# First-half memory values as 32-column strips on block-diagonal probabilities, in a 64-segment recurrent attention kernel

## The chip, the core and the metric

The kernel runs on one core of a Trainium2 chip. The metric is the device time of one execution in microseconds; the engines are named as in the profile: PE is TensorE (PEld its weight loads), DVE is VectorE, ACT is ScalarE, POOL is GpSimd, SP is SyncE.

## The reference

The input x has 2048 rows of 640. It is normalized, cut into 64 segments of 32 rows, and the segments are processed one after the other. Eight memory rows stand before the 32 rows of a segment, and the eight output rows of the memory become the memory of the next segment:

```python
for s in range(n_seg):
    h = concatenate([mem, xs])                  # 8 + 32 rows of 640
    q, k, v = h @ Wq, h @ Wk, h @ Wv            # 32 heads of 128
    scores = where(mask, q @ k.T * scale, -1e9) # memory rows see all 40, tokens are causal
    o = softmax(scores) @ v @ Wo
    mem = o[:, :8]; outs.append(o[:, 8:])
```

Behind it come a residual, a second layer norm, and a feed-forward part (640 to 1728 to 640) with a squared ReLU. All tensors are bf16.

## The kernel before

All weights lie in SBUF. The order of instructions is written out by hand, and each engine works through its own queue in that order. `step(b, sp)` is one segment s = 4b + sp, with four segments to a block of 128 rows. The last eight rows of each segment (the "tails") do not feed the recurrence through the projections of the segment's main part: their q, k and v are projected for four segments together as fill work, which stands in the list `fill` and is run in places where PE would wait. Other postponed work stands in the lists `late`, `mid` and `owed`; `run(list, n)` issues from them.

One step goes as follows on PE. The rows that matter (8 memory rows and 24 tokens, `hT4`) are projected with 32-column weight loads, four of them side by side in the array's columns (k = 0 to 3 on output partitions 32k): q and k of heads' half 0 and 1 (`project`), then v in two halves (`ps0`, `ps1`, from five 128-row pieces c = 0 to 4 each). ACT brings the results out of PSUM as rows (q, k) or into `v`; DVE turns the rows (`flip`) into `qT` and `kT`. `v` has partitions (g, key), with g one of four head groups, and columns (i, e), where i is one of eight heads of a group and e the head's 128 columns.

Attention is split. The memory's eight queries are on the recurrence: `scores(n)`, for half n (four of the eight i), lets all heads share one 128x40 score tile `sm` (partitions g, j, query; `spread` puts the queries into `qz` by POOL). `soft1(n)` takes the maximum on DVE and the exponential `em` with its sum `zm` on ACT. `soft2(n)` makes the probabilities on DVE: reciprocal `rm`, `pmem` = em times rm in two instructions (the 32 main keys, and the eight tail keys spread over four j by the mask `same`), and a 32x32-block transposition to `pTm`. `values(n)` multiplies: 16 matmuls with a 32-row weight load (one g's keys of one head, 128 columns) and eight moving columns, and four for the tails (`vt4`), into the PSUM tile `po`; `values_out(n)` copies the memory part into `oT` (DVE for half 0, ACT for half 1).

The tokens' attention is one segment late: `token_scores` puts 128x320 scores into a bank `sk`; DVE and ACT make the softmax during the second part of the step (`tk`, `ek`, `zk`); POOL scales it (`pkt`, `pk`); DVE turns it in the next step (`pTt`, `pTk`, from `owed[0]` and `owed[1]`); `token_values` of segment s-1 multiplies it in the same `po` tile, and ACT copies it out in the step after (`token_out`). `tokens_kept`, on POOL, puts the tails' part aside (`owed[2]`).

Then `wo_rounds` multiplies `oT` by Wo into `pw`, in 16 rounds of four matmuls; its first six rounds need the half 0 that `values_out(0)` wrote, and the rounds enclose `token_values` and `values(1)`. `mem_to_hT` turns the memory rows of `pw` into the next segment's `hT4`.

The order around the change, on PE: `scores(0)`; v half 0, c = 0, 1; `token_scores(0)`; v half 0, c = 2 to 4; v half 1, c = 0, 1; `scores(1)`; `token_scores(1)`; v half 1, c = 2; `values(0)`; v half 1, c = 3, 4; one fill unit; `wo_rounds` 0 to 6. On DVE: `mx` of half 0, two kT flips, `soft2(0)`, `mx` of half 1, the eviction of half 0, `soft2(1)`, then the tokens' softmax.

`matmul` (L116 in the profile, for every matrix product) counts PE's instructions in `issued`, and `align` splits some projections' matmuls in two, so that the count at a given place of a step is the same modulo 256.

Of the kernel before, what the change touches and what calls it, by code (L numbers as in the profile page):

```python
# [9 lines left out]
ALU = mybir.AluOpType  # L10
AX = mybir.AxisListType
F32 = mybir.dt.float32
BF16 = mybir.dt.bfloat16
# [3 lines left out]
def kernel(  # L17
# [28 lines left out]
    NS = S // SEG  # L46
    HD = 24
    TL = SEG - HD
    NK = SEG + M
# [11 lines left out]
    const = ctx.enter_context(tc.tile_pool(name="const", bufs=1))  # L61
# [13 lines left out]
    wv = wts.tile([128, DC * HE], BF16)  # L75
    wo = wts.tile([128, H, D], BF16)

    ident = const.tile([128, 128], BF16)
    o_ring = [const.tile([64, DH], BF16, name="o%d" % k) for k in range(5)]
    o0 = const.tile([128, DC, 32], BF16, name="om")  # L80
    nc.vector.memset(o0[:], 0.0)
    make_identity(nc, ident[:])
    mhalf = const.tile([128, 1], F32)
    nc.vector.memset(mhalf[:], -0.5)
# [13 lines left out]
        nc.vector.tensor_copy(out=same[r], in_=ident[r, r].rearrange("p (j k) -> p j k", k=TL))  # L98
    nc.vector.tensor_reduce(out=diag[:], in_=same[:], op=ALU.add, axis=AX.X)
    nc.vector.tensor_copy(out=same[:], in_=diag[:].unsqueeze(2).to_broadcast([128, 4, TL]))  # L100
    qT = const.tile([128, H, NK], BF16)
    kT = const.tile([128, H, NK], BF16)
    oT = const.tile([128, H, NK], BF16)
    nc.vector.memset(oT[:], 0.0)
# [9 lines left out]
    def matmul(*a, **k):  # L114
        issued[0] += 2
        nc.tensor.matmul(*a, **k)  # L116
# [136 lines left out]
    def evac(dve, out_, in_):  # L253
        if dve:
            nc.vector.tensor_copy(out=out_, in_=in_)
        else:
            nc.scalar.copy(out=out_, in_=in_)  # L257
# [15 lines left out]
    def wo_rounds(lhs, pw, h0, h1):  # L273

        for h in range(h0, h1):
            for kh in range(2):
                for ch in range(2):
                    j = kh * 2 + ch
                    p = h // 8 * 16 + kh * 8 + h % 8
                    matmul(pw[32 * j:32 * j + 32, 0:DH], lhsT=lhs(p), rhs=wov2[:, head(p), ch],  # L280
                                     start=(h == 0), stop=(h == 15))
# [17 lines left out]
        for a in range(2):  # L299
            nc.vector.tensor_tensor(out=hT4[64 * a:64 * a + 64, :, sp, 0:M], in0=tr[0:64, a, :, 0:M], in1=tc_[:, a], op=ALU.add)  # L300

    fill, late, mid, owed = [], [], [], [[], [], []]

    def run(q, n):
        while n > 0 and q:
            q.pop(0)()
            n -= 1
# [85 lines left out]

    def mem0_to_hT(hT4):
        mt = s1.tile([128, DC, 32], BF16, tag="pk", name="mt")
        nc.vector.transpose(out=mt[:], in_=o0[:])
        nc.vector.tensor_copy(out=hT4[:, :, 0, 0:M], in_=mt[:, :, 0:M])

    def tails_in(b, sp, which="qk", h0=0, h1=H):
# [23 lines left out]
    oTg = oT[:].rearrange("p (n g j) q -> p n g j q", n=2, g=G)  # L423
    back = []

    def token_values(s, v, vt4, po, opens):

        sp = s % 4
        pTk, pTx = back.pop()
        for i in range(HG):  # L430
            for g in range(G):
                r = slice(32 * g, 32 * g + 32)
                matmul(po[:, g, i * 32:(i + 1) * 32], lhsT=v[r, i * E:(i + 1) * E], rhs=pTk[r, i, :],
                                 start=(opens and i == 0), stop=False, skip_group_check=True)
        for u in range(2):
            for g in range(G):
                r = slice(32 * g, 32 * g + 32)
                matmul(po[:, g, u * 128:(u + 1) * 128].rearrange("p (j q) -> p j q", q=32)[:, :, HD:32],
                                 lhsT=vt4[r, sp, u, :], rhs=pTx[r, u], start=False, stop=True, skip_group_check=True)
# [17 lines left out]
    prev = {}  # L457

    def step(b, sp, v=None):
# [41 lines left out]
        def soft1(n):  # L501
            mx = s2.tile([128, 1], F32, tag="mx", name="mx")
            nc.vector.tensor_reduce(out=mx[:], in_=sms[n][:, 0:NK], op=ALU.max, axis=AX.X, negate=True)  # L503
            em = s2.tile([128, NK], BF16, tag="em", name="em")
            zm = s2.tile([128, 1], F32, tag="zm", name="zm")
            nc.scalar.activation(out=em[:], in_=sms[n][:, 0:NK], func=ACT.Exp, bias=mx[:, 0:1], scale=1.0,  # L506
                                 accum_out=zm[:])
            ems[n], zms[n] = em, zm

        def soft2(n):  # L510
            rm = s2.tile([128, 1], F32, tag="rm", name="rm")
            nc.vector.reciprocal(out=rm[:], in_=zms[n][:])
# [6 lines left out]
            nc.vector.transpose(out=pT[:], in_=pm[:])  # L519
            return pT  # L520

        def values(n, pT, po):
            c0 = 256 + n * 4 * M
            for j in range(4):
                i = n * 4 + j
                for g in range(G):
                    r = slice(32 * g, 32 * g + 32)
                    matmul(po[:, g, c0 + j * M:c0 + (j + 1) * M], lhsT=v[r, i * E:(i + 1) * E],
                                     rhs=pT[r, j * M:(j + 1) * M], start=(i == 0), stop=False,
                                     skip_group_check=True)  # L530
            for g in range(G):
                r = slice(32 * g, 32 * g + 32)
                matmul(po[:, g, c0:c0 + 4 * M], lhsT=vt4[r, sp, n, :], rhs=pT[r, 32:64],
                                 start=False, stop=True, skip_group_check=True)

        def values_out(n, po):
            c0 = 256 + n * 4 * M
            evac(n == 0, oTg[:, n, :, :, 0:M], po[:, :, c0:c0 + 4 * M].rearrange("p g (j m) -> p g j m", m=M))

        if not ready and not last:  # L540
            align(s + b, 4 * 8 * DC + 32 + 1 + 16)
# [12 lines left out]
        elif not ready:  # L554
            spread(1)
        run(late, 10)
        run(owed[2], 1)

        def first_half():
            if not last:  # L560
# [23 lines left out]
            proj(wv, "half", lhs, 0, ps0, 2, DC)  # L584
            nc.scalar.copy(out=v[:, 0:512], in_=ps0[:])
        if not last:
            pT0 = soft2(0)
        if not ready:
            ps1 = mmtile()
            proj(wv, "half", lhs, 1, ps1, 0, 2)  # L590
# [2 lines left out]
        token_scores(1)  # L593
        if not last:
            soft1(1)
        if ready:
            run(fill, DC)
        po = pop.tile([128, G, 512], F32, tag="po", name="po")
        if not ready:
            proj(wv, "half", lhs, 1, ps1, 2, 3)  # L600
        if not last:
            values(0, pT0, po)
            values_out(0, po)
        if not ready:
            proj(wv, "half", lhs, 1, ps1, 3, DC)
            nc.scalar.copy(out=v[:, 512:1024], in_=ps1[:])  # L606
        if not last and len(fill) > 7:
            run(fill, 1)
# [8 lines left out]
        pw = chn.tile([128, 512], F32, tag="ch", name="pw")  # L617
        main = lambda p: oT[:, p, 0:32]
        wo_rounds(main, pw, 0, 6)
        if s:  # L620
            token_values(s - 1, prev["v"], prev["vt4"], po, last)
        if not last:
            values(1, pT1, po)
            values_out(1, po)
        wo_rounds(main, pw, 6, 8)
        run(fill, DC if ready else 1)
        wo_rounds(main, pw, 8, 12)
# [32 lines left out]
        owed[1].append(lambda: nc.vector.transpose(out=pTk[:], in_=pk[:]))  # L660
        back.append((pTk, pTx))
        if not last:
            tails_in((s + 1) // 4, (s + 1) % 4)
# [242 lines left out]
    end_output(NS - 2)  # L906
    run(late, 100)
    po = pop.tile([128, G, 512], F32, tag="po", name="po")
    token_values(NS - 1, prev["v"], prev["vt4"], po, True)
    for n in range(2):  # L910
        token_out(n, po)
    tokens_kept(NS - 1)
# [102 lines left out]
```

## Time and profile before

| what | value |
|---|---|
| median of three runs | 959.4 us (959.19 to 960.17) |
| profiled execution | 958.06 us |
| its span, first to last instruction | 956.3 us |
| granted PE clock | 1.000 |
| PE busy | 929.1 us, 97% |
| DVE busy | 699.7 us, 73% |
| ACT busy | 548.4 us, 57% |
| POOL busy | 258.2 us, 27% |

A row of the groups gives line, engine, operation, tiles (out<-in), shape and count, then busy us, mean ns of one, and idle time just before. A row of the timeline gives start and duration in us, then the same names, the count of merged instructions, and in brackets an idle time of that engine and what ended it. A shape such as 128\*32 on PE is rows by columns of the loaded weights.

### The profile page before, as it was taken

Reading aid. Unit: us, or ns where it says so; the run is one execution under the profiler, and the core shown is the slowest. Engines: PE = TensorE matmul, PEld = TensorE weight load, DVE = VectorE, ACT = ScalarE, POOL = GpSimd, SP = SyncE. Lnnn points to the kernel's source line nnn. Section 1 sums busy time; section 2 is a strip of 40 time slices with the busy share of each in tenths; the row PEclk is TensorE's granted clock in tenths of the full one; section 3 lists DMA queues with packets and bytes.
Section 4 is the critical chain, followed back from the end, with each engine's and each line's share of the span. In section 5 each row is a group of like instructions: output and inputs, shape, how many; then the busy total and the mean of one; then the engine's idle time right before and its main releaser. Section 6 shows DMA issues by size and latency. Waiting matters only on the chain.

```text
span 956.3 us, 57547 instructions
## 1 busy us (share of the span) xinstructions
PE 929.1 (97%) x25874; PEld 570.3 (60%) x25883; DVE 699.7 (73%) x2136; ACT 548.4 (57%) x1343; POOL 258.2 (27%) x798
## 2 busy tenths in 40 slices
PE   4989999999999999999999999999999998999998
PEld 2545666666666666666666666656666665555555
DVE  3167778888888888888887787878787888566532
ACT  2556666666666666666666666656666665523321
POOL 1013222222222222222222222222222233263300
PEclk9999999999999999999999999999999999999999
DMA  9973210101010101010101010101010111643320
GB/s 360 396 235 90 45 29 13 29 13 30 10 33 9 34 10 34 9 34 9 33 10 34 9 32 11 32 11 32 11 32 11 53 43 21 199 113 86 94 56 28
DMA packets 60838, 56.74 MB, mean 59 GB/s; under 512 B 27696, under 2 KB 56752, under 8 KB 58672
## 3 DMA queue, kind: packets, MB, share of 16 engines
q1 hardware_dynamic: 59712, 52.73, 18.3%
q8 instruction: 202, 3.31, 1.5%
q10 hardware_dynamic: 880, 0.34, 0.1%
q14 instruction: 44, 0.36, 0.1%
HBM read 38.37 MB, written 9.44 MB: 50 GB/s over the span
## 4 chain that ended last, share of the span: by engine, by line
PE 93%; DMA 3%; DVE 2%; ACT 1%; issue 1%; ACTq 0%; DVEq 0%
PE ps L116 63%; PE pw L116 16%; PE y L116 6%; PE po L116 5%; DMA vt_d<-row 2%; PE sm L116 1%; PE pa L116 1%; DMA om<-in_A_mem_dram 1%; ACT otc L298 0%; ACTq L157 0%; ACT row L266 0%; DVE otr L297 0%; DVE kTt L269 0%; DVE qT L269 0%; DVE kT L269 0%
## 5 line engine op out<-in xcount | busy, mean ns | idle before, releaser
L116 PEld LDWEIGHTS <-hT 128*32 128x32 bf16 x8383 | 216.9, 96 | 146.2 <-DVE hT L300 20.7
L116 PE MATMUL pw<-wo,oT 128*32 128x320 bf16 x4224 | 178.4, 300 | 0.2
L116 PE MATMUL ps<-wv,hT 128*32 128x512 bf16 x2520 | 177.5, 380 | 0.0
L116 PE MATMUL ps<-wq,hT 128*32 128x512 bf16 (+1 forms) x3168 | 160.6, 336 | 4.8 <-DVE hT L300 4.8
L116 PE MATMUL ps<-wk,hT 128*32 128x512 bf16 (+1 forms) x2575 | 159.7, 375 | 0.0
L641 POOL TENSOR_TENSOR pkt<-ek,rk 128x64 bf16<-128x64 bf16 x64 | 19.3, 301 | 421.7 <-DVE rk L639 408.4
L116 PEld LDWEIGHTS <-oT 128*32 128x32 bf16 x4224 | 100.9, 96 | 44.8 <-ACT oT L257 9.1
L269 DVE STREAM_TRANSPOSE qT<-row 128x512 bf16<-128x512 bf16 x128 | 89.5, 699 | 24.4 <-ACT row L264 20.5
L264 ACT ACTIVATE row<-ps 128x512 bf16<-128x512 f32 (+1 forms) x170 | 93.7, 562 | 13.7 <-PE ps L116 11.7
L937 ACT ACTIVATE wv<-ps,b1f 128x512 bf16<-128x512 f32 (+1 forms) x56 | 37.6, 673 | 66.5 <-PE ps L116 66.0
L442 ACT CAST oT<-po 128x512 bf16<-128x512 f32 x128 | 74.7, 586 | 0.0
L298 ACT COPY otc<-otr 64x40 f32<-64x40 f32 x126 | 28.2, 224 | 71.5 <-DVE otr L297 71.1
L453 POOL COPY qz<-qT 128x96 bf16<-128x96 bf16 x126 | 33.5, 266 | 112.5 <-DVE mx L503 58.2
L116 PEld LDWEIGHTS <-hTt 128*32 128x32 bf16 x1640 | 45.1, 97 | 31.4 <-issue 2.0
L266 ACT CAST row<-ps 128x512 bf16<-128x512 f32 (+1 forms) x113 | 61.6, 560 | 1.9 <-PE ps L116 0.5
L635 DVE TENSOR_REDUCE zk<-ek 128x8 f32<-128x320 bf16 x64 | 31.1, 486 | 42.9 <-ACT ek L633 42.9
L116 PEld LDWEIGHTS <-v 32*128 32x128 bf16 x4064 | 42.1, 91 | 32.8 <-issue 18.4
L116 PE MATMUL y<-wq,wk 128*128 128x320 bf16 x448 | 61.2, 299 | 0.2 <-DVE wk L938 0.2
L484 ACT CAST row<-ps 128x256 bf16<-128x256 f32 x126 | 40.8, 376 | 30.3 <-PE ps L116 30.2
L257 ACT CAST oT<-po 128x128 bf16<-128x128 f32 x63 | 16.8, 267 | 65.3 <-PE po L116 65.3
L606 ACT CAST v<-ps 128x512 bf16<-128x512 f32 x63 | 37.0, 587 | 29.7 <-PE ps L116 29.7
L116 PEld LDWEIGHTS <-qz 128*32 128x32 bf16 x2016 | 36.0, 95 | 28.1 <-ACT em L506 1.9
(109 smaller groups left out, 1659.9 us busy)
## 6 DMA issues: line engine op xcount, KB each, us to landing
wv<-in_A_Wv_dram SPq DMA_DIRECT2D x5, 1024.0 KB
wq<-in_A_Wq_dram SPq DMA_DIRECT2D x5, 1024.0 KB
wk<-in_A_Wk_dram SPq DMA_DIRECT2D x5, 1024.0 KB
vt<-vt_d SPq DMA_DIRECT2D x60, 64.0 KB
xt<-in_A_x_dram SPq DMA_DIRECT2D x18, 160.0 KB
wo<-in_A_Wo_dram SPq DMA_DIRECT2D x2, 1280.0 KB
wo<-in_A_Wo_dram SPq DMA_DIRECT2D x4, 640.0 KB
wq<-in_B_w_dram SPq DMA_DIRECT2D x1, 2080.0 KB
```

Source lines behind the costliest of these rows:

```text
L116: nc.tensor.matmul(*a, **k)
L264: nc.scalar.mul(out=row, in_=ps, mul=scale)
L266: nc.scalar.copy(out=row, in_=ps)
L269: nc.vector.transpose(out=dst[:, n * 16:(n + 1) * 16, 0:32], in_=row.rearrange("p (h e) -> p h e", e=32))
L298: nc.scalar.copy(out=tc_[:, a], in_=tr[64:128, a, :, 0:M])
L442: nc.scalar.copy(out=oTg[:, n, :, :, M:NK], in_=po[:, :, n * 128:(n + 1) * 128].rearrange("p g (j q) -> p g j q", q=32))
L453: nc.gpsimd.tensor_copy(out=d.rearrange("p a (j f) -> p a j f", j=3)[:, :, :, 0:M], in_=src[:, :, 0:3, :])
L484: nc.scalar.copy(out=row[:, u * 256:(u + 1) * 256], in_=ps[:, u * 256:(u + 1) * 256])
L606: nc.scalar.copy(out=v[:, 512:1024], in_=ps1[:])
L635: nc.vector.tensor_reduce(out=zk[:], in_=ek[:], op=ALU.add, axis=AX.X)
L641: nc.gpsimd.tensor_tensor(out=pkt[:], in0=ek[:, :, SEG:NK], in1=rk[:].unsqueeze(2).to_broadcast([128, HG, TL]), op=ALU.mult)
L937: nc.scalar.activation(out=r[:, 0:w], in_=ps[:, 0:w], func=ACT.Relu, bias=b1f[:, fc:fc + 1], scale=1.0)
```

## The change

Half 0 of the memory values is computed the other way round. The probabilities are laid out block-diagonally over the four head groups: `soft2_wide` multiplies them by `gmask` and `gsame`, masks that keep column group g only on the partitions of group g, into `pwide` (128 x 2 x 4 x 32: main keys and tail keys). The main part is one DVE instruction; the tail part is two POOL instructions, the second of which scales by `rm`. One DVE transposition of 256 columns gives `pTwide`. `values_wide` then loads `v` with all 128 key partitions and 32 of a head's columns at a time, and multiplies 32 moving columns: 16 matmuls, and four for the tails with 128 moving columns. They write strips of 32 partitions into columns 320 to 447 of the bank `sk`, which holds the token scores in columns 0 to 319. Its eviction to `oT` stays on DVE.

Half 1 stays as it was and loses its argument n; `po` is taken later, ahead of `token_values`. In PE's order the values now come after c = 2 and 3 of v's half 1 instead of after c = 2. The turning of `pTk` moves from `owed[1]` to a new `owed[3]`, run behind `soft1(1)`; `tokens_kept` is run behind `soft2_wide`. The first memory rows are loaded into a part of `qT` instead of a tile of their own, one output buffer is dropped, and `issued` is corrected by two in some steps.

```diff
-    o_ring = [const.tile([64, DH], BF16, name="o%d" % k) for k in range(5)]
+    o_ring = [const.tile([64, DH], BF16, name="o%d" % k) for k in range(4)]
...
+    gmask = const.tile([128, 4], BF16)
+    nc.vector.tensor_reduce(out=diag[:], in_=ident[:].rearrange("p (g k) -> p g k", k=32), op=ALU.add, axis=AX.X)
+    nc.vector.tensor_copy(out=gmask[:], in_=diag[:])
+    gsame = const.tile([128, 4, 4 * TL], BF16)
+    nc.vector.tensor_tensor(out=gsame[:], in0=same[:].rearrange("p j k -> p (j k)").unsqueeze(1).to_broadcast([128, 4, 4 * TL]),
+                            in1=gmask[:].unsqueeze(2).to_broadcast([128, 4, 4 * TL]), op=ALU.mult)
...
+        def soft2_wide(n):
+            rm = s2.tile([128, 1], F32, tag="rm", name="rm")
+            nc.vector.reciprocal(out=rm[:], in_=zms[n][:])
+            pm = s1.tile([128, 2, 4, SEG], BF16, tag="pwide", name="pwide")
+            tails_ = pm[:, 1].rearrange("p g (j k) -> p (g j) k", k=TL)
+            nc.gpsimd.tensor_tensor(out=tails_, in0=ems[n][:, SEG:NK].unsqueeze(1).to_broadcast([128, 16, TL]),
+                                    in1=gsame[:].rearrange("p g (j k) -> p (g j) k", k=TL), op=ALU.mult)
+            nc.gpsimd.tensor_tensor(out=tails_, in0=tails_, in1=rm[:].unsqueeze(2).to_broadcast([128, 16, TL]), op=ALU.mult)
+            nc.vector.scalar_tensor_tensor(out=pm[:, 0], in0=ems[n][:, 0:SEG].unsqueeze(1).to_broadcast([128, 4, SEG]),
+                                           scalar=rm[:, 0:1], in1=gmask[:].unsqueeze(2).to_broadcast([128, 4, SEG]),
+                                           op0=ALU.mult, op1=ALU.mult)
+            pT = s1.tile([128, 2, 4, SEG], BF16, tag="pTwide", name="pTwide")
+            nc.vector.transpose(out=pT[:].rearrange("p t g k -> p (t g k)"), in_=pm[:].rearrange("p t g k -> p (t g k)"))
+            return pT
+
+        def values_wide(pT, sk):
+            c0 = HG * NK
+            split = lambda x: x.rearrange("p (g j m) -> p g j m", g=G, m=M)
+            main, kept = (pT[:, t].rearrange("p g k -> p (g k)") for t in range(2))
             for j in range(4):
-                i = n * 4 + j
+                for q in range(4):
+                    r = slice(32 * q, 32 * q + 32)
+                    matmul(split(sk[r, c0:c0 + 128])[:, :, j], lhsT=v[:, j * E + 32 * q:j * E + 32 * q + 32],
+                           rhs=split(main)[:, :, j], start=False, stop=False, skip_group_check=True)
+            for q in range(4):
+                r = slice(32 * q, 32 * q + 32)
+                matmul(sk[r, c0:c0 + 128], lhsT=vt4[:, sp, 0, 32 * q:32 * q + 32], rhs=kept,
+                       start=False, stop=True, skip_group_check=True)
+            evac(True, oTg[:, 0, :, :, 0:M], split(sk[:, c0:c0 + 128]))
...
-        run(owed[2], 1)
...
-            pT0 = soft2(0)
+            pT0 = soft2_wide(0)
+        run(owed[2], 1)
...
             soft1(1)
+        run(owed[3], 1)
...
-        po = pop.tile([128, G, 512], F32, tag="po", name="po")
         if not ready:
-            proj(wv, "half", lhs, 1, ps1, 2, 3)
+            proj(wv, "half", lhs, 1, ps1, 2, 4)
         if not last:
-            values(0, pT0, po)
-            values_out(0, po)
+            values_wide(pT0, sk)
+            issued[0] += 0 if sp else 2
         if not ready:
-            proj(wv, "half", lhs, 1, ps1, 3, DC)
+            proj(wv, "half", lhs, 1, ps1, 4, DC)
...
-        owed[1].append(lambda: nc.vector.transpose(out=pTk[:], in_=pk[:]))
+        owed[3].append(lambda: nc.vector.transpose(out=pTk[:], in_=pk[:]))
```

More of the change, by code (lines that the diff above doesn't have):

```diff
@@ L78 @@
     ident = const.tile([128, 128], BF16)
-    o_ring = [const.tile([64, DH], BF16, name="o%d" % k) for k in range(5)]
-    o0 = const.tile([128, DC, 32], BF16, name="om")
-    nc.vector.memset(o0[:], 0.0)
+    o_ring = [const.tile([64, DH], BF16, name="o%d" % k) for k in range(4)]
     make_identity(nc, ident[:])
@@ L100 @@
     nc.vector.tensor_copy(out=same[:], in_=diag[:].unsqueeze(2).to_broadcast([128, 4, TL]))
+    gmask = const.tile([128, 4], BF16)
[4 more added lines that the diff above has]
+                            in1=gmask[:].unsqueeze(2).to_broadcast([128, 4, 4 * TL]), op=ALU.mult)
     qT = const.tile([128, H, NK], BF16)
+    o0 = qT[:].rearrange("p h k -> p (h k)")[:, 0:DC * 32].rearrange("p (c f) -> p c f", f=32)
+    nc.vector.memset(o0, 0.0)
     kT = const.tile([128, H, NK], BF16)
@@ L300, in mem_to_hT @@
             nc.vector.tensor_tensor(out=hT4[64 * a:64 * a + 64, :, sp, 0:M], in0=tr[0:64, a, :, 0:M], in1=tc_[:, a], op=ALU.add)
-    fill, late, mid, owed = [], [], [], [[], [], []]
+    fill, late, mid, owed = [], [], [], [[], [], [], []]
     def run(q, n):
@@ L395, in mem0_to_hT @@
         mt = s1.tile([128, DC, 32], BF16, tag="pk", name="mt")
-        nc.vector.transpose(out=mt[:], in_=o0[:])
+        nc.vector.transpose(out=mt[:], in_=o0)
         nc.vector.tensor_copy(out=hT4[:, :, 0, 0:M], in_=mt[:, :, 0:M])
@@ L424, with token_values @@
     back = []
-    def token_values(s, v, vt4, po, opens):
+    def token_values(s, v, vt4, po):
         sp = s % 4
@@ L433, in token_values @@
                 matmul(po[:, g, i * 32:(i + 1) * 32], lhsT=v[r, i * E:(i + 1) * E], rhs=pTk[r, i, :],
-                                 start=(opens and i == 0), stop=False, skip_group_check=True)
+                                 start=(i == 0), stop=False, skip_group_check=True)
         for u in range(2):
@@ L520, in soft2, with values @@
             return pT
-        def values(n, pT, po):
-            c0 = 256 + n * 4 * M
-            for j in range(4):
-                i = n * 4 + j
+        def soft2_wide(n):
[16 more added lines that the diff above has]
+            main, kept = (pT[:, t].rearrange("p g k -> p (g k)") for t in range(2))
+            for j in range(4):
+                for q in range(4):
[7 more added lines that the diff above has]
+            evac(True, oTg[:, 0, :, :, 0:M], split(sk[:, c0:c0 + 128]))
+        def values(pT, po, opens):
+            c0 = 256 + 4 * M
+            for j in range(4):
+                i = 4 + j
                 for g in range(G):
@@ L528, in values @@
                     matmul(po[:, g, c0 + j * M:c0 + (j + 1) * M], lhsT=v[r, i * E:(i + 1) * E],
-                                     rhs=pT[r, j * M:(j + 1) * M], start=(i == 0), stop=False,
+                                     rhs=pT[r, j * M:(j + 1) * M], start=(opens and j == 0), stop=False,
                                      skip_group_check=True)
@@ L532, in values @@
                 r = slice(32 * g, 32 * g + 32)
-                matmul(po[:, g, c0:c0 + 4 * M], lhsT=vt4[r, sp, n, :], rhs=pT[r, 32:64],
+                matmul(po[:, g, c0:c0 + 4 * M], lhsT=vt4[r, sp, 1, :], rhs=pT[r, 32:64],
                                  start=False, stop=True, skip_group_check=True)
-        def values_out(n, po):
-            c0 = 256 + n * 4 * M
-            evac(n == 0, oTg[:, n, :, :, 0:M], po[:, :, c0:c0 + 4 * M].rearrange("p g (j m) -> p g j m", m=M))
+            evac(False, oTg[:, 1, :, :, 0:M], po[:, :, c0:c0 + 4 * M].rearrange("p g (j m) -> p g j m", m=M))
         if not ready and not last:
@@ L619, in step @@
         wo_rounds(main, pw, 0, 6)
+        po = pop.tile([128, G, 512], F32, tag="po", name="po")
         if s:
-            token_values(s - 1, prev["v"], prev["vt4"], po, last)
+            token_values(s - 1, prev["v"], prev["vt4"], po)
         if not last:
-            values(1, pT1, po)
-            values_out(1, po)
+            values(pT1, po, s == 0)
         wo_rounds(main, pw, 6, 8)
@@ L908 @@
     po = pop.tile([128, G, 512], F32, tag="po", name="po")
-    token_values(NS - 1, prev["v"], prev["vt4"], po, True)
+    token_values(NS - 1, prev["v"], prev["vt4"], po)
     for n in range(2):
```

## The prediction

> **What bounds the kernel now.** I read the page first, then the timeline of one segment around the changed step, then the groups by form for prices.
>
> The page's busy line and its chain:
>
> ```profile
> PE 929.1 (97%) x25874; PEld 570.3 (60%) x25883; DVE 699.7 (73%) x2136; ACT 548.4 (57%) x1343; POOL 258.2 (27%) x798
> ...
> PE 93%; DMA 3%; DVE 2%; ACT 1%; issue 1%; ACTq 0%; DVEq 0%
> ```
>
> TensorE carries the chain and works through its queue in order. Whatever holds its next instruction moves the end, once in each of 62 like segments of about 12 us (of 64; the first has no value projection, the last no memory).
>
> The timeline of one segment, from the first half's exponential to the first output matmuls (weight loads show when TensorE reaches each step):
>
> ```profile
> 516.66 0.29 ACT L506 ACTIVATE em<-sm,mx 128x40 bf16<-128x40 f32 x1
> ...
> 516.86 0.19 ACT L506 ACTIVATION_READ_ACCUMULATOR em<-sm,mx 128x1 f32 x1
> 517.09 0.15 DVE L512 RECIPROCAL rm<-zm 128x1 f32<-128x1 f32 x1
> ...
> 517.69 0.12 PEld L116 LDWEIGHTS <-hT 128*32 128x32 bf16 x4
> ...
> 517.70 0.24 DVE L519 STREAM_TRANSPOSE pTm<-pmem 128x64 bf16<-128x64 bf16 x1
> 517.87 0.16 DVE L503 TENSOR_REDUCE mx<-sm 128x1 f32<-128x40 f32 x1
> 518.04 0.17 PEld L116 LDWEIGHTS <-v 32*128 32x128 bf16 x16 [0.23 <-ACT v L585]
> ...
> 518.27 0.12 PEld L116 LDWEIGHTS <-hT 128*32 128x32 bf16 x8
> ...
> 518.41 0.29 DVE L255 CAST oT<-po 128x128 bf16<-128x128 f32 x1 [0.38 <-PE po L116]
> ...
> 518.76 0.54 PEld L116 LDWEIGHTS <-oT 128*32 128x32 bf16 x13 [0.15 <-DVE oT L255]
> ```
>
> To see: em ends at 517.05; probabilities, values, eviction and first oT load follow at 518.76, 1.71 later. pTm is ready (517.94) about when TensorE wants it (518.04), and TensorE already waits 0.15 for the eviction. So this chain of small steps is as tight as TensorE's own work; nothing spare lies in it. In three other timelines em's end to oT is 1.78, 1.67 and 1.72: mean 1.72.
>
> Prices of the new operations:
>
> ```profile
> L644 POOL TENSOR_TENSOR pk<-ek,rk 128x256 bf16<-128x256 bf16 x64 | 39.8, 622 | 0.0
> ...
> L660 DVE STREAM_TRANSPOSE pTk<-pk 128x256 bf16<-128x256 bf16 x64 | 25.8, 403 | 0.0
> ...
> L641 POOL TENSOR_TENSOR pkt<-ek,rk 128x64 bf16<-128x64 bf16 x64 | 19.3, 301 | 421.7 <-DVE rk L639 408.4 <-DVE hn L744 6.7 <-ACT otmp L287 6.6
> ```
>
> To see: one POOL product costs 301 ns at 64 columns and 622 at 256, so 408 by the straight line at 128; a 256-column transposition costs 403. The hand-overs are in the opening timeline:
>
> ```profile
> 3.95 0.21 DVE L175 BATCH_NORM_AGGREGATE lnmv<-lnst 128x2 f32<-128x12 f32 x1
> ...
> 4.25 0.22 POOL L177 TENSOR_SCALAR lnrs<-lnmv 128x1 f32<-128x1 f32 x1 [2.80 <-DVE lnmv L175]
> ...
> 4.56 0.60 POOL L178 TENSOR_TENSOR lnrs<-lnrs,mhalf 128x1 f32<-128x1 f32 x1
> ...
> 5.30 0.45 DVE L191 TENSOR_SCALAR xn<-xt,lnmv,lnrs 128x640 bf16<-128x640 bf16 x1
> ```
>
> To see: into POOL 0.09 (4.16 to 4.25), POOL to a dependent POOL instruction 0.09 (4.47 to 4.56), POOL to DVE 0.14 (5.16 to 5.30).
>
> **What TensorE saves.** Both forms of the first half's memory values are 20 weight loads and 20 matmuls. Now they cost more than their issue, because the 32-row tiles follow and precede 32-column tiles: from the c=2 group (517.69) to the c=3 group (518.27) is 0.58, where like groups of four stand 0.216 apart (twenty start at 500.59, the next at 501.67). So they cost 0.36. The new strips stay in the column form; sixteen qT loads of that form take 0.14 (517.55 to 517.69), and the four tail strips, which move 128 columns, a quarter of 0.216, so 0.19 in all. Saving 0.17 a segment, 10.5 us over 62, if TensorE had nothing to wait for. The Trainium skill (TensorEngine Tiling (Array Packing), Key Properties) says that changing the tiling mode drains the engine; these gaps agree, and by that rule alone the sum would be this 10.5 us gain.
>
> **What it waits for instead.** In the new order TensorE reaches the values after c=2 and c=3: 517.69 + 2 x 0.216 = 518.12. The probabilities must now go through POOL: masked tails (needs em only), tails times 1/sum (needs the first and rm), and DVE's 256-column transposition, which waits for POOL. From em's end 517.05: 0.09 into POOL, 0.41 first product, 0.09, 0.41 second, 0.14 to DVE, 0.40 transposition, 0.05 to TensorE (hT's end 511.37 to its load 511.42) = 1.59, so 518.64. TensorE stands 0.52. DVE's own masked main part (128 columns; the 32-column form costs 246) ends before POOL does and is off this path.
>
> Then values to eviction start 0.37 as now (518.04 to 518.41; twenty pairs both times) plus 0.04 for the wider tail strips, eviction 0.29, to the oT load 0.06: 519.40. From em's end 2.35, against 1.72 on average: **0.63 later** a segment. What TensorE saved and the work that it still has (c=4 and some fill, 0.43) lies inside this, before the eviction lands. Afterwards the order is as before and nothing gives time back: the recurrence (pw, otr, hT) starts from the later output matmuls.
>
> **Behind DVE's wait** are queued the second half's maximum (0.16), the moved pTk transposition (0.40) and the eviction. Laid end to end after 518.59 they let the eviction start at 519.15 instead of 519.05; neighbours on DVE overlap by some 0.08 each (518.62 starts before 518.70), so 0 to 0.10. I take 0 and keep 0.10 (6.2 us) for the range. The second half's probabilities end 1.06 after the eviction starts (543.28 to 544.34): 520.11, while TensorE wants them at 520.20 + 0.63. The token scores' softmax shifts with the eviction, as TensorE does; its sum ended 0.25 before otr started (510.06, 510.31), and still does.
>
> **Edits at nothing.** pTk's old place (515.08 in this segment) was covered: the qT flip behind it waits for its row from ACT (514.91 plus 0.60, flip at 515.54). Only where a layer-norm step follows pTk, in one segment of four, does the flip start some 0.2 earlier, and there em still waits for ACT's two kT rows. tokens_kept (0.40 on POOL) moves behind both products; POOL is then idle for over 6 us, and the next token eviction on ACT that waits for it comes 4 us later. The strips share the token scores' bank, which is released by DVE at the same instruction as before. The po tile is taken later and its old evictions are long done. No DMA is issued or moved; 34 more waits stand in TensorE's queue for landed vt4 tiles, each a few ns. The opening adds a 128x128 product on DVE ahead of xn at 12.53, which TensorE's transpositions await: 0.3, with the mask copy 0.4 once.
>
> **Sum.** 958.06 (the profiled execution; span 956.3) + 62 x 0.63 + 0.4 = 997.5. The median 959.4 is 1.3 above the profiled one: **999 us**.
>
> **Bounds.** POOL's spans may mislead: by starts, pkt to pk is 0.25 and pk to the next 0.56, so 0.36 at 128. With that for both and hand-overs 0.1 shorter in all the delay is 0.43: 986. At POOL's shortest span (0.22) for both products it is 0.25: 975. With 0.62 for both, 1.05: 1025. I take 0.41, between its two nearest forms.
>
> **Rivals.**
> Shared port, more delay: in the feed-forward part a DVE product of two SBUF tensors takes 0.42 alone and 1.63 when POOL's product began 0.05 earlier:
>
> ```profile
> 869.16 0.42 DVE L938 TENSOR_TENSOR wk<-wv 128x512 bf16<-128x512 bf16 x1
> ...
> 869.97 1.39 POOL L749 TENSOR_TENSOR wv<-wk,wq 128x640 f32<-128x640 bf16 x1
> ...
> 870.02 1.63 DVE L938 TENSOR_TENSOR wk<-wv 128x512 bf16<-128x512 bf16 x1
> ```
>
> It ended 0.29 after POOL. Here DVE's masked main part (em and the mask, both in SBUF) would meet POOL's first product, end 0.29 after it at 517.84, and hold off the second (due 517.64) by 0.20: delay 0.83, **1011**. Against: the blocked one may give way before its end. The Trainium skill (SBUF — State Buffer, Who interferes with whom) has this as an exclusive lock held for the whole instruction; the two rows agree. Chance, with the DVE queue's 0.10 (1005): 0.22.
>
> POOL cheaper than its spans: 975 to 986, chance 0.2. POOL dearer (0.62 each): 1025, chance 0.05.
>
> Faster: TensorE's 0.17 counts because the probabilities come in time: 958.06 - 10.5 + 0.4 + 1.3 = **949**. It decides at 518.12: the transposition must reach TensorE 1.07 after em's end, where my sum has 1.59 and the floor of two shortest POOL products 1.21. Even then eviction and oT would come at 518.88, 0.12 after now (967), unless they shorten too. For it: the 0.36 is real. Chance 0.04.
>
> The change does nothing: the built order on each engine shows all of it, so only cancelling would give 959; chance 0.01.
>
> **Numbers.** 999 has 0.48 (988 to 1005). With the shared port and the dear end of the cheap case the range is 975 to 1015, leaving out the rest. A difference under 0.2% (1.9 us) can't be told here. Faster 0.04, same 0.02, slower 0.94.
>
> **What would show it.** Right: pTwide's transposition starting about 1.1 after em's end; TensorE idle about 0.5 ahead of its first strip; the eviction about 0.6 later than now; a group pwide<-em on POOL near 0.41; segments of 12.6. Wrong: strips starting at 517.69 + 0.43 on that scale without idle time, POOL products near 0.2, or the oT load less than 1.9 after em's end.

## The result and the profile after

The changed kernel takes 986.86 us (median of four runs, 986.29 to 987.22) against 959.3 us for the kernel before (four runs, 957.73 to 960.17): a ratio of 1.0289, with a 95% interval of 1.0271 to 1.0306. It is slower by 27.6 us. The profiled execution took 987.11 us with a span of 985.3 us, 29.0 more than the span before, at a granted clock of 1.000.

The busy line and the chain of the page after:

```profile
PE 939.2 (95%) x25858; PEld 564.3 (57%) x25867; DVE 720.3 (73%) x2076; ACT 546.5 (55%) x1343; POOL 307.1 (31%) x924
...
PE 76%; ACT 8%; DVE 5%; POOL 5%; DMA 2%; issue 2%; ACTq 0%; POOLq 0%; DVEq 0%
```

TensorE fell from 93% to 76% of the chain. POOL, which was not in it at all, now holds 5%, and ACT (ahead of POOL, with two kT rows and `em`) and DVE (behind it, with `pTwide`) grew. In the segment shown below the chain leaves TensorE once and goes through the softmax of half 0.

The timeline of one segment after, of the same kind as the one shown of before, from the end of the exponential to the first output matmuls:

```profile
534.81 0.19 ACT L512 ACTIVATION_READ_ACCUMULATOR em<-sm,mx 128x1 f32 x1
...
535.14 0.40 POOL L533 TENSOR_TENSOR pwide<-em,gsame 128x128 bf16<-128x128 bf16 x1 [0.46 <-ACT em L512]
...
535.23 0.46 DVE L536 SCALAR_TENSOR_TENSOR pwide<-em,rm,gmask 128x128 bf16<-128x128 bf16 x1
...
535.62 0.40 POOL L535 TENSOR_TENSOR pwide<-pwide,rm 128x128 bf16<-128x128 bf16 x1
535.65 0.15 PEld L122 LDWEIGHTS <-hT 128*32 128x32 bf16 x8
...
536.05 0.45 DVE L540 STREAM_TRANSPOSE pTwide<-pwide 128x256 bf16<-128x256 bf16 x1 [0.37 <-POOL pwide L535]
...
536.55 0.28 PE L122 MATMUL ps<-pTwide,v 128*32 128x32 bf16 x16 [0.27 <-DVE pTwide L540]
536.55 0.17 PEld L122 LDWEIGHTS <-v 128*32 128x32 bf16 x15 [0.58 <-issue]
...
536.94 0.29 DVE L261 CAST oT<-ps 128x128 bf16<-128x128 f32 x1
...
537.28 0.67 PEld L122 LDWEIGHTS <-oT 128*32 128x32 bf16 x24 [0.46 <-DVE oT L261]
537.29 1.00 PE L122 MATMUL pw<-wo,oT 128*32 128x320 bf16 x24
```

`em` ends at 535.00. The two POOL products follow each other (535.14 to 535.54, 535.62 to 536.02), the transposition starts 0.03 behind the second and ends at 536.50, and the strips start at 536.55. TensorE took up c = 2 and 3 at 535.65; at 0.216 a group it was through with them at 536.08, and the strips came 0.47 later. (The matmul records, whose ends are modelled, leave 0.27 of idle time; the weight side shows 0.58, since the first strip's weights had been loaded ahead.) The first oT load comes 2.28 after `em`'s end, where it was 1.71.

The same two last steps in the kernel before, from its timeline of that segment (`em` ended at 517.05), with the matmuls, which the prediction did not look at:

```profile
518.76 0.82 PEld L116 LDWEIGHTS <-oT 128*32 128x32 bf16 x24 [0.15 <-DVE oT L255]
...
518.92 0.99 PE L116 MATMUL pw<-wo,oT 128*32 128x320 bf16 x24
```

Before, the load ran 0.16 ahead of its matmul, because the array still had the fill unit's four matmuls to do, which started at 518.71; after, load and matmul come together (537.28, 537.29), because those four had started at 536.93. Measured to the first output matmul, the change costs 2.29 - 1.87 = 0.42 in this segment, while the loads say 0.57. Over all segments the medians of this stretch are, by place in a block of four, 1.88, 1.88, 1.88 and 1.76 before and 2.41, 2.29, 2.29 and 2.29 after: 0.41 more in the second and third place, 0.53 in the first and fourth, 0.48 on average.

The groups by form after, for the new operations:

```profile
L540 DVE STREAM_TRANSPOSE pTwide<-pwide 128x256 bf16<-128x256 bf16 x63 | 28.1, 445 | 23.7 <-POOL pwide L535 23.7
L536 DVE SCALAR_TENSOR_TENSOR pwide<-em,rm,gmask 128x128 bf16<-128x128 bf16 x63 | 27.5, 437 | 2.2
L535 POOL TENSOR_TENSOR pwide<-pwide,rm 128x128 bf16<-128x128 bf16 x63 | 25.2, 400 | 5.2 <-DVE pwide L536 0.4
L533 POOL TENSOR_TENSOR pwide<-em,gsame 128x128 bf16<-128x128 bf16 x63 | 25.2, 400 | 30.1 <-ACT em L512 29.3 <-DVE rm L530 0.8
```

The POOL products cost 400 ns each, as estimated (408). DVE waits 23.7 us in all for the second of them, 0.38 on average in 63 segments.

Where the 29.0 us of the profiled spans lie: 27.3 between the first and the last hand-over of the memory (62 segments, 0.44 each), 1.4 before the first hand-over, 0.3 behind the last. The median length of a segment, by its place in a block of four (from the end of one hand-over to the next, from segment 16 on), shows the loss in every place:

| kernel | first | second | third | fourth |
|---|---|---|---|---|
| before | 12.44 | 11.96 | 11.92 | 11.91 |
| e3, the moves only | 12.32 | 11.96 | 11.92 | 11.90 |
| after | 12.86 | 12.37 | 12.34 | 12.44 |
| e1, tails on DVE | 12.76 | 12.20 | 12.16 | 12.26 |
| e2, no tails | 12.49 | 11.93 | 11.90 | 12.00 |
| e7, transposition split | 12.49 | 12.14 | 12.11 | 12.21 |
| e5, row form on a constant | 12.32 | 11.96 | 11.92 | 11.90 |
| e6, strips on a constant | 12.45 | 11.77 | 11.73 | 11.73 |
| e9, the same with the count mended | 12.40 | 11.77 | 11.73 | 11.72 |

The first place needs care. In the profiled execution of the kernel before, its segments scatter from 12.32 to 12.80; in e3, whose time equals that of the kernel before, their median is 12.32. Against e3 the change loses 0.54, 0.41, 0.42 and 0.54, which is the 0.53, 0.41, 0.41 and 0.53 of the stretch from `em` to the first output matmul, and 0.48 on average. The 0.44 above is smaller mainly because that one execution of the kernel before had longer first segments.

### The profile page after: what moved, and what is told of

It reads as the page before. It is cut to its first block, busy times and chain, and to the rows that moved or that the text cites. A ratio compares the mean times of both kernels' runs of the same rounds, so it can differ in the third digit from the quotient of the medians.

```text
span 985.3 us, 57590 instructions
## 1 busy us (share of the span) xinstructions
PE 939.2 (95%) x25858; PEld 564.3 (57%) x25867; DVE 720.3 (73%) x2076; ACT 546.5 (55%) x1343; POOL 307.1 (31%) x924
## 4 chain that ended last, share of the span: by engine, by line
PE 76%; ACT 8%; DVE 5%; POOL 5%; DMA 2%; issue 2%; ACTq 0%; POOLq 0%; DVEq 0%
PE ps L122 49%; PE pw L122 16%; PE y L122 6%; ACT row L490 4%; PE po L122 4%; DVE pTwide L540 3%; POOL pwide L535 3%; POOL pwide L533 2%; ACT em L512 2%; DMA vt_d<-row 1%; PE pa L122 1%; DMA qT<-in_A_mem_dram 1%; DVE wk L971 0%; ACT row L272 0%; ACT otc L304 0%
## 5 line engine op out<-in xcount | busy, mean ns | idle before, releaser
L122 PEld LDWEIGHTS <-oT 128*32 128x32 bf16 x4224 | 95.9, 96 | 60.0 <-DVE oT L261 25.7
L122 PEld LDWEIGHTS <-v 32*128 32x128 bf16 (+1 forms) x4064 | 47.5, 92 | 58.7 <-issue 53.6
L970 ACT ACTIVATE wv<-ps,b1f 128x512 bf16<-128x512 f32 (+1 forms) x56 | 37.5, 672 | 66.9 <-PE ps L122 65.6
L512 ACT ACTIVATE em<-sm,mx 128x40 bf16<-128x40 f32 x126 | 37.0, 293 | 55.3 <-DVE mx L509 53.7
L275 DVE STREAM_TRANSPOSE kT<-row 128x512 bf16<-128x512 bf16 x65 | 45.5, 700 | 11.1 <-ACT row L272 11.0
```

The costliest lines, as they stand in the source:

```text
L275: nc.vector.transpose(out=dst[:, n * 16:(n + 1) * 16, 0:32], in_=row.rearrange("p (h e) -> p h e", e=32))
L970: nc.scalar.activation(out=r[:, 0:w], in_=ps[:, 0:w], func=ACT.Relu, bias=b1f[:, fc:fc + 1], scale=1.0)
```

## The experiments

Theory: each segment's loss is the way of the tail probabilities through POOL, two products in a row and a transposition that waits for them; the strips themselves cost TensorE less than the row form, but that saving lies inside the wait. The rivals are these: the moved `pTk` or `tokens_kept` does it; DVE's product, slowed by POOL's, does it; the values' new form costs something of its own.

**e1: the tails' two POOL products as one DVE product.**

```diff
-            nc.gpsimd.tensor_tensor(out=tails_, in0=ems[n][:, SEG:NK]..., in1=gsame[:]..., op=ALU.mult)
-            nc.gpsimd.tensor_tensor(out=tails_, in0=tails_, in1=rm[:]..., op=ALU.mult)
+            nc.vector.scalar_tensor_tensor(out=tails_, in0=ems[n][:, SEG:NK]..., scalar=rm[:, 0:1],
+                                           in1=gsame[:]..., op0=ALU.mult, op1=ALU.mult)
```

> The changed kernel with the two POOL products for the tail keys replaced by one DVE instruction (em times 1/sum times mask, 128 columns), so that no hand-over to POOL and back is left. Late-probabilities theory: after rm the two DVE products and the transposition follow each other and the transposition ends about 0.25 earlier than in the changed kernel, so 62 x 0.25 = 15 us less: about 972. DVE-queue theory (what costs is the moved pTk transposition and the other work on DVE ahead of the eviction): DVE gets more work, so 987 or more. Strip theory (the strips themselves cost TensorE more than the row form): 987.

It took 975.86 us against 956.45 for the kernel before on the same chip: 1.0200 (1.0185 to 1.0216). So 10 of the 29 us go when POOL is left out, where 15 were expected; a loss by DVE's queue or by the strips themselves would have left 987 or more. The groups by form of this kernel:

```profile
L533 DVE SCALAR_TENSOR_TENSOR pwide<-em,rm,gsame 128x128 bf16<-128x128 bf16 x63 | 22.2, 352 | 2.2
L536 DVE SCALAR_TENSOR_TENSOR pwide<-em,rm,gmask 128x128 bf16<-128x128 bf16 x63 | 21.8, 346 | 0.0
```

The two DVE products stand one behind the other and the transposition starts 0.88 after `em`'s end, where it was 1.05; the first output matmul comes at 2.11 instead of 2.29. The saving is about as large as the shorter way (62 x 0.18 = 11), and no larger; the expectation had taken the transposition to come 0.25 earlier, and it came 0.17 earlier. The row of L536 shows something else: the same instruction took 437 ns while POOL worked beside it, and 346 here (352 in e2, again without a POOL product).

**e2: no tail products at all.** This leaves out the tail keys of half 0: `pwide` is a constant tile of zeros, of which only the main half is written.

```diff
+    pwz = const.tile([128, 2, 4, SEG], BF16)
...
-            nc.gpsimd.tensor_tensor(out=tails_, ...
-            nc.gpsimd.tensor_tensor(out=tails_, ...
+            pm = pwz
```

> The changed kernel with the tail products left out (the tail keys' probabilities of half 0 stay zero, so half 0 of the memory lacks them); TensorE still multiplies all strips. Chain: rm, one DVE product, the 256-column transposition. Late-probabilities theory: pTwide is there about when TensorE arrives, the wait of 0.5 goes, and the time falls by about 0.45 a segment to 959 to 961, about the time before; it does not fall to 949, because values, eviction and oT load still follow one another. TensorE-work theory (the saving in the array counts fully once nothing waits): 949. Strip theory: 980 or more.

It took 961.21 us, 1.0049 (1.0032 to 1.0065) of the kernel before. The timeline of one segment of this kernel:

```profile
519.12 0.19 ACT L514 ACTIVATION_READ_ACCUMULATOR em<-sm,mx 128x1 f32 x1
...
519.93 0.45 DVE L538 STREAM_TRANSPOSE pTwide<-pwz 128x256 bf16<-128x256 bf16 x1
...
520.43 0.28 PE L124 MATMUL ps<-pTwide,v 128*32 128x32 bf16 x16
...
520.82 0.29 DVE L263 CAST oT<-ps 128x128 bf16<-128x128 f32 x1
...
521.16 1.00 PE L124 MATMUL pw<-wo,oT 128*32 128x320 bf16 x24
```

The strips come 0.05 behind the transposition, and without idle time on TensorE ahead of them. From `em`'s end (519.31) to the first output matmul it is 1.85, where the kernel before has 1.87. So about 25 of nearly 30 us are the tails' way. Of the 5 that remain, about 1 lies before the first hand-over, and most of the rest in the first and fourth places (0.17 and 0.10 a segment against e3). But nothing is won either: without any wait for the strips, TensorE then waits for the eviction (strips to eviction 0.39, eviction 0.29), and the chain from `em` to `oT` is as long as the old one. The saving on TensorE does not appear in the time.

**e3 and e4: the two moves by themselves.** e3 is the kernel before with `pTk` and `tokens_kept` moved as in the change; e4 is the changed kernel with both moved back.

```diff
-        run(owed[2], 1)
...
+        run(owed[2], 1)          # behind soft2(0)
...
+        run(owed[3], 1)          # behind soft1(1)
...
-        owed[1].append(lambda: nc.vector.transpose(out=pTk[:], in_=pk[:]))
+        owed[3].append(lambda: nc.vector.transpose(out=pTk[:], in_=pk[:]))
```

> The kernel before with only the moves: pTk turned after the second half's maximum, tokens_kept after the first half's probabilities. Late-probabilities theory: pTk ends about when the eviction wants to start, so 959 to 962. DVE-queue theory: most of the added 27 us are here, 975 or more.

> The changed kernel with pTk turned at its old place and tokens_kept at its old place. Late-probabilities theory: 985 to 990, since em still waits for ACT and the eviction for TensorE; tokens_kept ahead of POOL's first product may add up to 0.1 a segment (993). DVE-queue theory: back to 965 or less.

e3 took 956.2 us, 0.9998 (0.9988 to 1.0007) of the kernel before; e4 took 986.08, 1.0307 (1.0292 to 1.0323). The moves cost nothing and give nothing, in either kernel (e3 was expected at 959 to 962, and e4 has the ratio that the changed kernel has in e8).

**e5: does the row form wait for its probabilities?** The kernel before, with `values(0)` reading a constant tile of zeros instead of the probabilities of half 0.

```diff
-            values(0, pT0, po)
+            values(0, pTc, po)
```

> The kernel before with the first half's values taken from a constant tile of zeros instead of pTm (pTm is still computed, nobody reads it; half 0 of the memory's attention output is zero). It takes away only the wait for the probabilities. Drain theory (the row form waits until the 32-column matmuls have left the array): within 0.2% of the kernel before, 955 to 957 against 956.5. If the probabilities were what TensorE waited for, up to 0.1 a segment less: 950.

It took 955.5 us, 0.9983 (0.9974 to 0.9993) of the kernel before. With the probabilities always there, the weight loads of c = 2 and c = 3 still stand 0.57 apart (515.49 and 516.06 in one segment), as they did before (0.58). So the 0.36 around the row-form values is not a wait for `pTm`. How much of it is the change between the two tile forms can be estimated from half 1 of the same kernel, where the row form follows the row form. Its loads in the kernel before:

```profile
520.20 0.22 PEld L116 LDWEIGHTS <-v 32*128 32x128 bf16 x16
...
520.34 0.12 PEld L116 LDWEIGHTS <-vt 32*128 32x128 bf16 x4
```

Sixteen loads take 0.14 there, and the eight tail loads just ahead of them 0.05 (520.15 to 520.20), so twenty pairs take about 0.17 by themselves. The other 0.19 of the 0.36, an estimate, stands at the two changes of form.

**e6: what do strips save where they need not wait?** The kernel before, with the strips on a constant tile of zeros in the place of `values(0)`, behind c = 2. The strips go to the bank `sk`, so half 1 and the token values open the `po` tile.

```diff
-            values(0, pT0, po)
-            values_out(0, po)
+            values_wide(pTc, sk)
```

> The same with the strips: the kernel before, its own soft2 still computed and unread, with the strip form multiplying a constant tile of zeros into the token scores' bank at the old place after c = 2 (half 0 of the memory's attention output is zero). Against e5_row_const only the form of the matmuls differs. If the strips save TensorE 0.17 a segment once nothing waits: 946 to 949. If the saving is lost in the eviction and the oT load behind it as in e2_no_tails: 954 to 957. If strips cost more in themselves: over 960.

It took 951.37 us, 0.9937 (0.9921 to 0.9953) of the kernel before: 5.5 us less, and 4.1 us less than e5, from which only the form of the matmuls differs. 946 to 949 was expected. The weight loads of one segment, from its timeline:

```profile
514.91 0.12 PEld L118 LDWEIGHTS <-hT 128*32 128x32 bf16 x4
...
515.12 0.19 PEld L118 LDWEIGHTS <-v 128*32 128x32 bf16 x16
...
515.22 0.12 PEld L118 LDWEIGHTS <-vt 128*32 128x32 bf16 x4
...
515.25 0.17 PEld L118 LDWEIGHTS <-hT 128*32 128x32 bf16 x8
```

From c = 2 to c = 3 it is 0.34 where it was 0.58. In the second to fourth segments of a block 0.18 to 0.19 arrives in the time. In the first it does not (12.45 against 12.32 in e3 and e5), and some of these are up to 0.9 longer; this is why the saving is 5.5 us and not the 11 that 62 x 0.18 would be.

**e7: the same computation with the transposition in two.** The main half is turned as soon as DVE has written it; the tail half is turned behind the second half's maximum, and its four strips come behind c = 4.

```diff
-            nc.vector.transpose(out=pT[:]..., in_=pm[:]...)
+            turn(0)
...
             soft1(1)
+            turn0(1)
...
             # values_wide, between the main and the tail strips
+            proj(wv, "half", lhs, 1, ps1, 4, DC)
+            nc.scalar.copy(out=v[:, 512:1024], in_=ps1[:])
```

> The changed kernel with the transposition in two: the main keys are turned as soon as DVE's product is there, the tail keys after the second half's maximum, and on TensorE c = 4 stands between the 16 main strips and the 4 tail strips. Nothing is left out. Late-probabilities theory: the main strips come in time, the tail strips about 7.15 after the segment's start instead of 7.34, and the eviction 0.2 to 0.25 earlier: 970 to 975. If only the total work on DVE counts (one instruction more): 987 to 990.

It took 970.71 us against 956.84, 1.0146 (1.0131 to 1.0161): half of the loss is gone with POOL's products still there. Its timeline:

```profile
526.42 0.28 PE L122 MATMUL ps<-pTwide,v 128*32 128x32 bf16 x16
...
526.75 0.24 PE L122 MATMUL ps<-pTwide,vt 128*32 128x128 bf16 x4
...
527.04 0.29 DVE L261 CAST oT<-ps 128x128 bf16<-128x128 f32 x1
...
527.39 1.00 PE L122 MATMUL pw<-wo,oT 128*32 128x320 bf16 x24 [0.18 <-DVE oT L261]
```

`em` ended at 525.33. The main strips run 1.09 later (1.55 in the changed kernel); the tail strips, 1.42 later, are now what the eviction waits for, and the first output matmul comes at 2.06. Each half of 128 columns costs 312 ns to turn against 445 for the 256 together, so splitting is not free, but the second turning starts while the main strips are still to come (526.39, against 526.42). The kernel before is still faster by 13.9 us.

**e8: the changed kernel again, beside e5 to e7.**

> The changed kernel itself beside these, for the comparison on one chip: 984 to 988, 27 to 30 above the kernel before by every theory.

It took 986.21 us, 1.0308 (1.0291 to 1.0326).

**e9: e6 with the instruction count mended.** The change corrects the count of TensorE's instructions by two in the first step of each block. e6 had left that out, which could have kept the saving out of just those segments; this kernel adds it.

```diff
             values_wide(pTc, sk)
+            issued[0] += 0 if sp else 2
```

> e6_strip_const with the correction of TensorE's instruction count that the changed kernel also has (two in the first segment of each block). In e6_strip_const three of four segments were 0.18 shorter than before, and the first of each block was up to 0.9 longer, where the count that align keeps had drifted by 2 a block. If that drift hid the saving: 62 x 0.18 = 11 us below the kernel before, 945 to 948 against 957. If the first segments lose for another reason: 950 to 952, as e6_strip_const.

It took 949.49 us against 955.19, 0.9935 (0.9918 to 0.9951), the same saving as e6. The first segments of the blocks still show none (12.40, against 12.32 in e3 and e5). So the count is not why. The trace shows another cause. The strips' loads in one first segment of this kernel:

```profile
298.36 0.19 PEld L118 LDWEIGHTS <-v 128*32 128x32 bf16 x16
...
298.61 0.13 PEld L118 LDWEIGHTS <-vt 128*32 128x32 bf16 x4
```

The tail loads come 0.25 behind the first main load, where it is 0.10 in the other places (515.12 to 515.22 in the segment of e6 above). Between them, two instructions that only wait for semaphores stand in TensorE's queue (298.43 and 298.54), and the first tail load waits for a further one. These three wait for the four transfers of the block's new `vt4` tile, which were issued from 258.03 to 260.04 and had landed by 263.3: what costs time is not the transfer but passing the waits. A strip reads all 128 partitions of `vt4` and so needs the transfers of all four head groups at once; in the row form each load needs those of one group, and there the first place shows no such gap (0.095, as in the others). Every kernel here with strips has the gap, 0.16 to 0.20 once a block (0.13 in e7), and e2, e6 and e9 evict 0.17 to 0.18 later in the first place. In the changed kernel this is part of the 0.53 of its first segments. So 0.17 of the missing 0.18 is accounted for. No run takes these waits away, so what they cost is read from the traces alone; and why the first segments of e6 and e9 are longer still, up to 0.9 in e6, stays open.

## Why the prediction was right, and where its sum was off

The sign and the mechanism held: TensorE stands ahead of the strips, because the tails' probabilities come late through POOL and the transposition. The time, 986.86, lies in the range of 975 to 1015, but 1 us below the band of 988 to 1005 that had the most weight. It falls next to the 986 of a cheaper POOL largely by luck: that case supposed products of 0.36, which took 0.40, and it too counted to the load. Its shorter hand-overs did come (0.07 of the 0.1). Of the signs named, the transposition started 1.05 behind `em` (about 1.1), TensorE stood 0.47 (about 0.5), and the eviction came 0.58 later (about 0.6).

The sum was 12 us too high. Against the two profiled executions, 11.8 of this lies in the delay (62 x 0.63 = 39.1, measured 27.3) and 1.6 in the step from the profiled execution to the median; the opening and the end take 1.3 back.

**The delay of 0.63 a segment was mis-sized; it is 0.42 in the segment shown, and 0.44 (against the profiled execution of the kernel before) to 0.48 (against e3) on average.** There are two errors in the same direction:

- The end point. The prediction ended its chain at the first oT weight load and compared it with the load before. That load was no mark of TensorE's place: it had run 0.16 ahead of its matmul. Of the delay, 0.15 only used up this lead. The row that would have told it, the matmul at 518.92, stood in the same timeline. This is the larger error: by the loads, the mean of all segments is 2.32 after against 1.72 before, or 0.61, close to the 0.63; by the matmuls it is 0.48.
- The steps. From `em`'s end to the load was 2.28, not 2.35. Into POOL it was 0.14 instead of 0.09, and the transposition took 0.45 instead of 0.40 (the price was taken from `pTk`'s); but POOL to DVE was 0.03 instead of 0.14, the hand-over between the POOL products 0.08, the products 0.40, and the strips to eviction 0.39 instead of 0.41. None is large, and together they leave 0.07. On average over the segments only 0.03 of it is left, since the first segment of each block has the wait for `vt4`.

0.63 less 0.15 less 0.07 is 0.41; the segment shown has 0.42, because its load came 1.71 behind `em` before, and not the mean of 1.72. The prediction also said that nothing gives time back later; from the oT load to the token values' first load it was 1.08 before (518.76 to 519.84) and 0.93 after (537.28 to 538.21), which is the same 0.15 seen from the other side.

**POOL at 0.41.** Right: 400 ns. The line through its two nearest forms was the better of the estimates, and the difference of starts (0.36) was not.

**TensorE's saving of 0.17, unreachable.** Both right, but for the first segments of the blocks. e6 and e9 give 0.18 to 0.19 in the other places, where strips need not wait; e2 shows that, with the real probabilities of the main keys alone, the chain of softmax, strips, eviction is already as long as the old one. The faster rival's condition, a transposition done 1.07 after `em`'s end, was met in e2 but for the hand-over (519.31 to 520.38), and the time was 961, not 949: as the prediction had it for that case (967), the eviction came last. The Trainium skill (TensorEngine Tiling (Array Packing), Key Properties) has a change of the tiling mode drain the engine; e5 agrees, with the 0.57 that stays when the probabilities are constant, and so does the estimate of 0.19 for the changes of form, out of half 1.

**The shared port did not act on the path.** The rival had DVE's masked product blocked until POOL's first ended, and POOL's second held until DVE's ended. DVE's was stretched, from 346 to 437 ns, and ended at 535.69, 0.15 after POOL's first; but POOL's second started at 535.62, 0.08 behind its first, and took the same 400 ns. The Trainium skill (SBUF — State Buffer, Who interferes with whom) describes an exclusive lock for the whole instruction; the two overlapping spans here do not agree with a full block. The two rows of the feed-forward part come near it, though not exactly: the DVE product ended 0.29 behind POOL's, where a full block would leave all of its 0.42.

**DVE's queue.** The 0 that was taken is right: the maximum and `pTk` end at 536.93 and the eviction starts at 536.94, 0.39 behind the strips. `pTk`'s move left only 0.01 to spare, but the strips set this start: it is also 0.39 in e4 and e6, where `pTk` is turned at its old place.

**Edits at nothing.** e3 and e4 bear this out for the two moves. It was wrong for the 34 more waits on `vt4`, taken at a few ns each: the changed kernel has 126 instructions on TensorE's queue that only wait, the kernel before 92, and where two of them stand ahead of the tail strips, in the first segment of each block, these come 0.16 to 0.20 later (e9 above). With 0.17 this would be 2.6 us over 15 blocks, an estimate.

**Opening.** 0.4 was too little: 1.4 in the profiled execution, and 0.7 to 1.2 in the profiles of five other kernels that carry the new masks. The place scatters, though: the first hand-over ends at 64.9 to 65.6 with the masks, and at 63.0 to 64.2 in the five kernels without them. In the profiled execution a wait for the first memory rows' transfer was 6.2 us instead of 5.1; how much of the rest is the masks was not taken apart. The median of before, 1.3 above its profiled execution, also did not carry over: the profiled execution of the changed kernel is 0.25 above its median.

**Slower in every place.** This held. The forecast segment of 12.6 was for the shown kind (11.92 to 11.96 before); it is 12.34 to 12.37.

## What to carry to other kernels

A saving on the busiest engine counts only from the moment at which its operands are there: before costing it, follow the chain from the last common event (here the end of the exponential) to the next thing that the recurrence needs, in both orders, and see which chain ends last. Take matmuls, not weight loads, as the marks of TensorE's place: here a load ran 0.16 ahead of its matmul while the array had work queued. Where a small part of a result takes the long way (here eight of forty keys, through two POOL products), try its own transposition and its own matmuls, so that the large part need not wait for it; e7 took half of the loss away by that, though it stayed slower than the kernel before.

## What the runs showed of the hardware

- A DVE product of two SBUF operands took 437 ns with a POOL product beside it, and 346 to 352 without one. The POOL product beside it took 400 ns, as did the next one, which it hardly overlapped (0.07 us in the segment shown). So the contention here was partial and one-sided.
- Turning 32x32 blocks on DVE cost 312 ns for 128 columns and 403 to 445 for 256; the same shape differed by 10% between tiles (`pTk` 403 in the kernel before, 423 in the changed one; `pTwide` 445). Why is open.
- Twenty small matmuls in the row form, set between groups of the column form, take 0.36 us of TensorE with their operands ready, and 0.12 (0.34 - 0.216) in the column form by the weight loads of e6.
- In the segment shown, POOL to DVE was handed over in 0.03 us (0.14 in the opening of the kernel before), ACT to POOL in 0.14, one POOL instruction to a dependent one in 0.08.
- Two instructions that only wait, on TensorE's queue and for transfers that had landed some 35 us before, together with a wait on the load behind them, put that load 0.16 to 0.20 us back (0.13 in e7).
